# Five more filler products on TensorE ahead of the first running sum of a fused linear-attention and low-rank-mixer kernel

## The chip, the cores and the metric

The kernel runs on one NeuronCore of one Trainium2 chip. The metric is the device time of one execution in microseconds. Before the change, three timed runs gave 158.94, 158.34 and 158.42 us, so the median is 158.42 us.

## The reference

The reference is two layers in a row. The first is a gated linear attention over 4 batches, 8 heads, 768 time steps and a head size of 48:

```
state = alpha[:, :, t, :, None] * state + einsum('bhd,bhe->bhde', k[:, :, t], v[:, :, t])
y[:, :, t] = einsum('bhd,bhde->bhe', q[:, :, t], state)
```

Its output, with the heads side by side, is x of shape 4 x 768 x 384. The second layer is a mixer with a low rank over time and an MLP over channels:

```
h = x.transpose(0, 2, 1) @ U @ V          # rank 32 over the 768 time steps
u = x + h.transpose(0, 2, 1)
out = u + maximum(u @ w_ch1, 0) @ w_ch2   # 384 -> 1536 -> 384
```

## The kernel before, in words

Time is cut into chunks of 128 steps, six for each batch. In a chunk the recurrence over time becomes products. ScalarE (ACT) takes the logarithm of alpha (line 380), TensorE (PE) adds the logarithms up along time with triangular matrices (the running sum, f_cum, lines 387 to 399), ACT takes the exponentials of the sum and of its negative (lines 403 to 405), and GpSimd (POOL) or VectorE (DVE) scale k and q by these (line 411). PE then transposes k and q (line 428), ACT or DVE copy the transposed tiles out of PSUM (lines 277 and 279), PE forms the scores (line 452), DVE masks them (line 463), PE forms the state (lines 478 and 486) and the output y (lines 525 and 535). Batch 0 and most of batch 1 work on pairs of chunks in this way; the others have the same steps at lines 551 to 687. After the six chunks of a batch come the low-rank mix (lines 702 to 736) and the two products of the MLP (lines 765 and 791), with their relu (lines 775 and 777) and the last addition (line 797). The running sum is five lines of products: 384 columns (line 389), twice 192 (lines 390 and 391), 8 (line 392) and four times 4 (line 396).

The order of all this is not that of the loops. The loops only register operations, and Plan.run (line 125) issues them in the order of a table of three letters for each entry: two letters for the number of the operation and one for the engine that does it. Each engine works through its own instructions in that order, and waits on the others through semaphores. The queue of a DMA is that of the engine named by the letter, SyncE (SP) or ACT, so an ACT instruction behind a DMA that ACT issues waits until that DMA has been issued. The loads of alpha, k, q and v (line 350) fill 40 slots, and the first of them go out on both queues in turn with the first instructions.

An entry that begins with "++" is not an operation. Its third letter is a count of fillers, A for 0, B for 1, and so on:

```
for _ in range(CODE.index(table[n + 2])):
    self.warm(x)
```

A filler (line 270) is a product of 128 x 128 by 128 x 512 that reads a tile of zeros, set by DVE at line 201, and writes a PSUM bank that nothing holds at that point of the table; nobody reads its result. Ten such products are spread over the first part of the kernel, each entry with a count of one. Two of these entries, numbers 1 and 10 of the table, stand ahead of entry 11, the running sum of the first chunk (operation 141). Between them lie loads on SP and ACT, the preload of ACT's table and the logarithm of the first alpha tile.

Of the kernel before, what the change touches and what calls it, by code (L numbers as in the profile page):

```python
# [13 lines left out]

CODE = "ABCDEFGHIJKLMNOPQRSTUVWXYZabcdefghijklmnopqrstuvwxyz0123456789+-"
TABLE = """
ArA++BAASAvSA-AA3SQPAAySAsSCLA++BCNPAtSAzA++BA5ACOACPAAwS++BCiADSAECAAxSBAACRGAuS++BCSGCjACQACkPA4SClA++BCmAA7ADUPDVADWA
A0SC5ACTPCoGCUPCWABDSDXAEEPEGAA6SCpDA9ACVDCxPC7P++BCnACMAC9AAFGC+ABBSDrAA2SCyDCqPCsDCaPBHSCbDCXPCzPEFAA8SCrPCYDDtPCtAA1S
CcPCZDCeP++BCdDC8ADYGDaPCuPDZDCfPEIGDcAC-GDTGCwDEKPEHAAJPDbPC0DBCABFSABSDhPGCAAKADwA++BChACvDDiPDdDDjDEJGDvADuAA+SDePDgD
AGPELPAHADkPEMDC1PDfDBEAENABGSC2PBLSC3DDyGD0PD2ABISCgDBJSBKSBPSGEPDlDC6GGGADIPDJPDKDEOPDxGDLPDAGGHAEDGDBPC4DDzPDnPERPEPD  # L20
# [836 lines left out]
```

## Time and profile before

| what | us |
|---|---|
| median of the three timed runs | 158.42 |
| lowest and highest of them | 158.34, 158.94 |
| span of the profiled execution, first to last instruction | 156.8 |
| PE busy in that span | 148.8 (95%) |
| DVE, ACT, POOL busy | 107.6, 90.0, 61.4 |

The profile gives no time of its execution beside the span; the median of the timed runs is 1.6 us above it. Times in the trace count from the first instruction. In a row of the timeline the first number is the start, the second the time from the start of the first instruction of the row to the end of the last, then come engine, line, operation and the tiles written and read, the number of instructions as x2, and in brackets how long the engine had stood idle and what released it. Products of PE overlap: the next one starts before the result of the one before is complete, so the distance between two starts says more of the pace than the duration of one.

### The profile page before, as it was taken

To read this page: it belongs to the slowest core of one execution; us is meant where nothing else is said; L and a number is where in the kernel's file an instruction comes from. 1 tells how busy PE (TensorE), PEld (TensorE's weight loads), DVE (VectorE), ACT (ScalarE), POOL (GpSimd) and SP (SyncE) were. 2 spreads that over 40 slices of the span, in tenths; PEclk is the share of its full clock that TensorE was granted. 3 is DMA by queue.
4 is the path that set the end of the run, shared out by engine and by line. 5 is a ranking of instruction groups with operands and counts; after the bars stand their busy time and mean duration, and the time that the engine had idled before them with its cause. 6 is when DMAs were issued, how large, how long until landed. Compare 5 with 4: busy or idle time off the path is not lost.

```text
span 156.8 us, 4413 instructions
## 1 busy us (share of the span) xinstructions
PE 148.8 (95%) x1715; PEld 97.7 (62%) x1715; DVE 107.6 (69%) x236; ACT 90.0 (57%) x234; POOL 61.4 (39%) x95
## 2 busy tenths in 40 slices
PE   2878999999999999999999999999999999999992
PEld 0456678666767656666668666665667555556662
DVE  6038899987899628816588976885989580673162
ACT  3678889986978272999958585379232202450000
POOL 8285995756088600136679261052623000000000
PEclk9999999999999999999999999999999999999999
DMA  5999999999988989989989996897976346345625
GB/s 145 319 323 326 268 301 313 344 265 268 280 239 193 270 161 191 189 169 211 208 169 214 134 222 119 169 181 145 176 144 151 105 87 139 127 129 151 199 100 201
DMA packets 98291, 31.53 MB, mean 201 GB/s; under 512 B 91968, under 2 KB 98240, under 8 KB 98272
## 3 DMA queue, kind: packets, MB, share of 16 engines
q1 hardware_dynamic: 92464, 29.11, 80.6%
q10 hardware_dynamic: 5808, 2.16, 5.2%
q8 instruction: 13, 0.21, 0.6%
q14 instruction: 6, 0.05, 0.1%
HBM read 23.79 MB, written 4.72 MB: 182 GB/s over the span
## 4 chain that ended last, share of the span: by engine, by line
PE 84%; DMA 8%; DVE 4%; ACT 1%; issue 1%; ACTq 0%; DVEq 0%
PE ps L791 30%; PE ps L765 29%; DMA io<-in_alpha_dram 8%; PE ps L716 3%; PE ps L620 3%; PE ps L592 2%; PE ps L687 2%; PE ps L428 2%; PE ps L535 2%; PE ps L558 2%; PE ps L682 1%; PE ps L736 1%; PE ps L452 1%; PE ps L643 1%; PE ps L702 1%; DVE rkq L411 1%
## 5 line engine op out<-in xcount | busy, mean ns | idle before, releaser
L791 PE MATMUL ps<-w_sb,h1t 128*128 128x384 bf16 (+2 forms) x300 | 53.1, 319 | 0.0
L765 PE MATMUL ps<-uT,w_sb 128*128 128x384 bf16 x288 | 51.0, 326 | 0.1
L775 ACT ACTIVATE h1t<-ps 128x384 bf16<-128x384 f32 x58 | 27.2, 509 | 19.1 <-PE ps L765 19.0
L791 PEld LDWEIGHTS <-h1t 128*128 128x128 bf16 x300 | 27.3, 97 | 15.9 <-issue 0.6
L765 PEld LDWEIGHTS <-w_sb 128*128 128x128 bf16 x288 | 27.0, 98 | 16.3 <-issue 0.4
L777 DVE TENSOR_SCALAR h1t<-ps 128x384 bf16<-128x384 f32 x38 | 20.1, 552 | 19.4 <-PE ps L765 15.9
L579 POOL TENSOR_TENSOR rkq<-io,aa 128x384 bf16<-128x384 f32 x12 | 11.7, 975 | 23.0 <-ACT aa L569 13.2
L630 DVE TENSOR_TENSOR pm<-ps,maskc 128x512 bf16<-128x512 f32 x28 | 17.7, 681 | 2.8 <-PE ps L620 2.8
L717 DVE TENSOR_TENSOR ub<-xb,ps 128x384 bf16<-128x384 bf16 x24 | 12.2, 549 | 6.9 <-PE ps L716 6.9
L797 DVE TENSOR_TENSOR io<-ub,ps 128x384 f32<-128x384 bf16 (+2 forms) x25 | 12.9, 531 | 3.7 <-PE ps L791 3.6
L277 ACT CAST xb<-ps 128x192 bf16<-128x192 f32 (+1 forms) x21 | 8.2, 393 | 10.6 <-PE ps L687 7.9
L463 DVE TENSOR_TENSOR pm<-ps,maskp 128x512 bf16<-128x512 f32 x20 | 13.2, 682 | 0.5 <-PE ps L452 0.2
L277 ACT COPY kqt<-ps 128x512 bf16<-128x512 bf16 x18 | 10.5, 608 | 1.6 <-PE ps L428 0.8
L579 POOL TENSOR_TENSOR rkq<-io,ai 128x384 bf16<-128x384 f32 x9 | 8.2, 914 | 6.9 <-PE ps L643 3.9
L411 POOL TENSOR_TENSOR rkq<-io,ai 128x384 bf16<-128x384 f32 x9 | 8.5, 945 | 6.1 <-ACT lt L380 3.1
L568 ACT ACTIVATE ai<-ps 128x384 bf16<-128x384 f32 x14 | 7.0, 502 | 5.6 <-PE ps L560 3.1
L654 POOL TENSOR_TENSOR st<-sm,tot 128x384 bf16<-128x384 f32 x8 | 6.9, 868 | 8.2 <-DVE sm L670 8.0
L571 ACT ACTIVATE tot<-ps,off 128x4 f32<-128x4 f32 x22 | 5.6, 279 | 5.3 <-PE ps L560 3.4
L279 DVE COPY kqt<-ps 128x512 bf16<-128x512 bf16 x18 | 7.3, 417 | 1.4 <-PE ps L592 0.9
L428 PE MATMUL ps<-ident,rkq 128*128 128x128 bf16 x80 | 8.0, 228 | 0.1
L281 POOL CAST w_sb<-h1t 128x384 bf16<-128x384 f32 x14 | 6.8, 516 | 2.9 <-DMA h1t<-in_moe_w_ch_dram 2.9
L411 POOL TENSOR_TENSOR rkq<-io,aa 128x384 bf16<-128x384 f32 x7 | 6.4, 910 | 3.4 <-ACT aa L404 2.3
(111 smaller groups left out, 224.5 us busy)
## 6 DMA issues: line engine op xcount, KB each, us to landing
io<-in_v_dram SPq DMA_DIRECT2D x22, 192.0 KB, 4.1
io<-in_q_dram SPq DMA_DIRECT2D x22, 192.0 KB, 4.4
io<-in_k_dram SPq DMA_DIRECT2D x21, 192.0 KB, 4.0
io<-in_alpha_dram SPq DMA_DIRECT2D x20, 192.0 KB, 4.3
out_dram<-io SPq DMA_DIRECT2D x13, 192.0 KB, 2.0
h1t<-in_moe_w_ch_dram SPq DMA_DIRECT2D x4, 576.0 KB, 6.0
h1t<-in_moe_w_ch_dram SPq DMA_DIRECT2D x3, 768.0 KB, 6.6
out_dram<-io SPq DMA_DIRECT2D x20, 96.0 KB, 2.2
```

What stands on the lines that cost most here:

```text
L277: nc.scalar.copy(dst, src)
L411: eng.tensor_tensor(jh(dst()[:, :, 0:D]), raw(a), jh(x()), op=ALU.mult)
L428: nc.tensor.matmul(dst, lhsT=ring()[:, HP * j + 2 * a : HP * j + 2 * a + 2, :].rearrange("t h w -> t (h w)"), rhs=ident, start=True, stop= ...
L463: nc.vector.tensor_tensor(dst, s2, maskp.to_broadcast([C, 2, 2, C]), op=ALU.mult)
L579: eng.tensor_tensor(dst()[:, :, 0:D], a(), x(), op=ALU.mult)
L630: nc.vector.tensor_tensor(pm()[:, :, par, :], s2, maskc.to_broadcast([C, HP, C]), op=ALU.mult)
L717: P.add(f"u {b}.{c}", lambda e, c=c, hb=hb: nc.vector.tensor_tensor(ub()[:, c, :], xb()[:, c, :], hb()[:, 0:DM], op=ALU.add), r=[hb] + xk( ...
L765: nc.tensor.matmul(hb()[:, 0:TW], lhsT=w1_sb[:, ct, jt * 128 : (jt + 1) * 128], rhs=u_half(uT, ct, tt, b in QUEUE_U), start=(ct == 0), sto ...
L775: nc.scalar.activation(dst, hb()[:, 0:TW], AF.Relu)
L777: nc.vector.tensor_scalar_max(dst, hb()[:, 0:TW], 0.0)
L791: nc.tensor.matmul(hb()[:, 0 : hi - lo], lhsT=h1()[:, jt, c * C : (c + 1) * C], rhs=w2_sb[:, jt, lo:hi], start=(jt == 0), stop=(jt == NJ - 1),
L797: P.add(f"out_{hi - lo} {b}.{c}", lambda e, hb=hb, lo=lo, hi=hi: nc.vector.tensor_tensor(flat(ou)[:, lo:hi], ub()[:, c, lo:hi], hb()[:, 0 ...
```

## The change

One letter of the table changes, the count of entry 1 from B (1) to G (6). PE therefore issues six fillers there in place of one, and with the one of entry 10 seven in place of two, ahead of the first running sum. Entries, order, engines, slots and every other count stay.

```
 TABLE = """
-ArA++BAASAvSA-AA3SQPAAySAsSCLA++BCNPAtSAzA++BA5ACOACPAAwS
...
+ArA++GAASAvSA-AA3SQPAAySAsSCLA++BCNPAtSAzA++BA5ACOACPAAwS
...
```

More of the change, by code (lines that the diff above doesn't have):

```diff
@@ L16 @@
 TABLE = """
-ArA++BAASAvSA-AA3SQPAAySAsSCLA++BCNPAtSAzA++BA5ACOACPAAwS++BCiADSAECAAxSBAACRGAuS++BCSGCjACQACkPA4SClA++BCmAA7ADUPDVADWA
+ArA++GAASAvSA-AA3SQPAAySAsSCLA++BCNPAtSAzA++BA5ACOACPAAwS++BCiADSAECAAxSBAACRGAuS++BCSGCjACQACkPA4SClA++BCmAA7ADUPDVADWA
 A0SC5ACTPCoGCUPCWABDSDXAEEPEGAA6SCpDA9ACVDCxPC7P++BCnACMAC9AAFGC+ABBSDrAA2SCyDCqPCsDCaPBHSCbDCXPCzPEFAA8SCrPCYDDtPCtAA1S
```

## The prediction

> **What bounds the kernel now.** I read the chain of waits first, then the timeline of PE around the added products, then the other engines' timelines at the places where PE waits, and last the busy times by stretch.
>
> ```profile
> span 156.8 us, 4413 instructions
> PE   2878999999999999999999999999999999999992
> PEclk9999999999999999999999999999999999999999
> PE 84%; DMA 8%; DVE 4%; ACT 1%; issue 1%; ACTq 0%; DVEq 0%
> ```
>
> PE is the bound of the kernel as a whole, with 84% of the chain. But the change sits in the first slices, where PE's digits are lowest, so what it is worth is read from there. There the chain is this, in order of time:
>
> ```profile
> 0.73 2.96 DMA io<-in_alpha_dram
> 3.73 4.70 DMA io<-in_alpha_dram
> 8.45 0.37 ACTq L350
> 8.98 4.45 DMA io<-in_alpha_dram
> 13.45 0.03 ACT lt L380
> 13.88 0.47 ACT ai L403
> 14.36 0.48 ACT kqt L277
> 14.88 0.38 PE ps L270
> ```
>
> Three loads of alpha follow one another. The load that starts at 8.98 is held back by an issue on ACT's queue at 8.45, which went out when the load before it had landed (3.73 + 4.70 = 8.43). No piece of PE's work is on the chain before 14.88. PE's own view of the same time:
>
> ```profile
> 1.19 1.04 PE L270 MATMUL ps<-h1t 128*128 128x512 bf16 x2 [1.19 <-DVE h1t L201]
> 4.30 0.48 PE L389 MATMUL ps<-lt,upto 128*128 128x384 bf16 x1 [2.07 <-ACT lt L380]
> 5.07 1.44 PE L270 MATMUL ps<-h1t 128*128 128x512 bf16 x3
> 6.58 0.48 PE L389 MATMUL ps<-lt,upto 128*128 128x384 bf16 x1
> 7.35 0.59 PE L270 MATMUL ps<-h1t 128*128 128x512 bf16 x1
> 7.73 0.53 PE L389 MATMUL ps<-lt,upto 128*128 128x384 bf16 x1
> 8.05 0.37 PE L390 MATMUL ps<-lt,below 128*128 128x192 bf16 x1
> 8.55 1.25 PE L428 MATMUL ps<-ident,rkq 128*128 128x128 bf16 x8
> 9.59 0.48 PE L389 MATMUL ps<-lt,upto 128*128 128x384 bf16 x1
> 9.91 0.25 PE L390 MATMUL ps<-lt,below 128*128 128x192 bf16 x1
> 9.99 0.25 PE L391 MATMUL ps<-lt,upto 128*128 128x192 bf16 x1
> 10.88 0.34 PE L486 MATMUL ps<-rv,rkq 64*128 64x96 bf16 x8 [0.54 <-POOL rkq L411]
> 11.44 0.32 PE L389 MATMUL ps<-lt,upto 128*128 128x384 bf16 x1 [0.21 <-ACT lt L380]
> 11.60 0.24 PE L390 MATMUL ps<-lt,below 128*128 128x192 bf16 x1
> 11.91 0.38 PE L270 MATMUL ps<-h1t 128*128 128x512 bf16 x1
> 12.13 0.38 PE L428 MATMUL ps<-ident,rkq 128*128 128x128 bf16 x4
> 12.84 0.34 PE L486 MATMUL ps<-rv,rkq 64*128 64x96 bf16 x8 [0.33 <-ACT rv L277]
> 14.03 0.32 PE L389 MATMUL ps<-lt,upto 128*128 128x384 bf16 x1
> ```
>
> Two things are to be seen. First, PE's pace doubles at 9.9. The 384 columns of line 389 take 0.32 from start to next start at 7.73 (to 8.05) and 0.16 at 11.44 (to 11.60); the 192 columns of line 390 take 0.08 at 9.91 (to 9.99). The clock digits of the page show 9 in every slice and hide this; the spacing is what I go by. Second, after 9.9 PE waits three times in three microseconds, for POOL, for the logarithm and for a cast of v on ACT. It isn't the engine that is late there. The ones that are:
>
> ```profile
> 5.25 0.49 ACT L403 ACTIVATE ai<-ps 128x384 bf16<-128x384 f32 x1 [1.00 <-PE ps L396]
> 6.00 1.35 ACT L380 ACTIVATE lt<-io 128x384 bf16<-128x384 f32 x3
> 8.86 0.51 ACT L277 CAST rv<-io 128x384 bf16<-128x384 f32 x1 [1.52 <-DMA io<-in_alpha_dram]
> 13.45 0.52 ACT L380 ACTIVATE lt<-io 128x384 bf16<-128x384 f32 x1 [0.21 <-DMA io<-in_alpha_dram]
> 9.91 0.91 POOL L411 TENSOR_TENSOR rkq<-io,ai 128x384 bf16<-128x384 f32 x1 [0.78 <-ACT ai L403]
> ```
>
> ACT ends its three logarithms at 7.35 and then stands until the issue at 8.45 lets it go on at 8.86. From there POOL waits for ACT, and PE for POOL and ACT. The stretches, 3.4 us wide (a width of my choice that parts the time at the change of pace), and the end of the kernel:
>
> ```profile
> 3.07:6.48 3.41, 2.18 (x11) 0.99 (x11) 0.93 (x8) 1.76 (x5) 1.21 (x6) 1.00 1.14 313
> 6.49:9.89 3.40, 3.28 (x27) 2.20 (x26) 0.00 (x0) 1.88 (x7) 1.77 (x2) 1.00 1.17 323
> 9.91:13.31 3.40, 2.32 (x52) 1.83 (x51) 2.03 (x5) 3.33 (x11) 2.92 (x3) 1.00 1.17 324
> 153.26:156.67 3.41, 0.72 (x12) 0.53 (x9) 0.86 (x2) 0.00 (x0) 0.00 (x0) 1.00 0.56 200
> 156.70:156.78 0.08, 0.00 (x0) 0.00 (x0) 0.00 (x0) 0.00 (x0) 0.00 (x0) 0.50 0.00 0
> ```
>
> The columns are the stretch and its length, then busy time of PE, of PE's weight load, DVE, ACT and POOL, the granted clock, the DMA share and GB/s. ACT is busy 3.33 of 3.40 us between 9.91 and 13.31, and the DMAs move 323 to 324 GB/s on both sides of the change of pace. So this start is set by loads and, from 8.86 on, by ACT.
>
> **The change part by part.**
>
> *The five products.* At the slow pace 384 columns take 0.32, so 512 take 0.32 x 512 / 384 = 0.43. Two products from 1.19 leave PE free at 1.19 + 2 x 0.43 = 2.05; seven at 1.19 + 7 x 0.43 = 4.20. The first running sum starts at 4.30 because the logarithm is ready then, so 0.10 is left: 5 x 0.43 = 2.15 us of new work in an idle gap. Cost to the sum: 0. The bounds: should the sum have to wait for the seventh result (the lone filler at 7.35 takes 0.59, so 1.19 + 6 x 0.43 + 0.59 = 4.36), it starts 0.06 late. Exponentials and logarithms on ACT would shift by as much, ending at 7.41, still 1.04 ahead of the issue at 8.45; without that cover it would cost 0.06. The products issue no DMA and add no wait, and their bank and their tile of zeros are those of the old ones.
>
> *The pace of what follows.* The change of pace at 9.9 comes after a stretch in which PE was busy 3.28 of 3.40 us, and not after one with 2.18 of 3.41. With five more products the second becomes 2.18 plus the filled part of the gap (3.07 to 4.20, 1.13), about 3.3, as full as the one that was followed by the fast pace. I take it that the pace doubles some 3.4 us earlier, near 6.5. What that takes from PE: the running sums at 6.58 and 7.73 last 0.77 (to 7.35) and 0.82 (to 8.55), against 0.47 at 11.44 (to 11.91): 0.65 saved. The filler lasts 0.38 (7.35 to 7.73) against 0.22 (11.91 to 12.13): 0.16. Eight transposes last 1.04 (8.55 to 9.59); at half of it 0.52 is saved. The 384 columns at 9.59: 0.16. Together 1.5 us of PE time. The bounds are 0 (pace unchanged) and 2.8, half of the 5.6 us between 4.30 and 9.91.
>
> *Where that goes.* None of it reaches the end, because of the line at 10.88: there PE stands 0.54 for POOL's scaled k. POOL got its exponential late (0.78 idle at 9.91), since ACT was stopped until 8.86 by the load of alpha. ACT's input from PE at that time, the running sum of the second pair, is there at 7.35 already at the slow pace. So PE's idle time before 10.88 grows from 0.54 to about 2.0, while the start at 10.88 stays, and with it 11.44, 12.84 and 14.03. Of the 1.5 us the path gets 0. Without the cover it would get all of it.
>
> *The sum.* 156.8 + 0 + 0 = 156.8 us of span. The timed median lies 158.42 - 156.8 = 1.6 above the span, for which the profile gives nothing; added back, it makes 158.4.
>
> **The rivals.**
>
> *The early pace reaches the end.* If some step after 13.45 ends last because of PE's slow work before 9.9, up to 1.5 us come back: 158.4 - 1.5 = 156.9, at the outer bound 155.6. For it speaks that PE is 84% of the chain, so any PE time truly freed is worth its full length. Against it stand the three waits after 9.9, each on an engine that is behind the loads. A timed run in which the fast pace comes later than 9.9 would bear it out better: then the slow products would fall on 11.44 to 14, where the idle times are only 0.21 and 0.33. The Trainium skill, "TensorE: Matmul & The Clock Gate", Part 1, gives this a reason: there the array's clock is halved until one window of about 3.4 us was busy, and the windows run freely, not from the kernel's start. By that rule the moment differs from run to run; the trace's doubling after a full stretch agrees, and one execution can't show the spread.
>
> *The fast pace is lost again: slower.* Faster products leave PE idler between 6.5 and 10.9, and the slow pace could return. At the end of the trace the granted clock is 0.50 after a stretch in which PE was busy 0.72 of 3.41 us; it stayed full through one with 2.32. After the change the stretch from 6.49 has about 3.28 - 1.5 = 1.8, between the two and nearer to 2.32, so I expect it kept. The point of decision is somewhere between 0.72 and 1.8. If it is lost, the products from 9.91 to 13.31 take up to twice their 2.32 us; idle times of 0.54 + 0.21 + 0.33 = 1.08 cover part, and 2.32 - 1.08 = 1.2 remain: 159.6. The skill's same page, section "HAM oscillation", warns of gaps over about 3.4 us before the next burst; the longest gap after 6.5 would here be the 2.0 us before 10.88, so by that rule the clock stays.
>
> *The products do not bring the pace forward.* They multiply zeros, and no row shows that such products count towards the change of pace; the stretch with 3.28 was mostly real work. Then the pace still doubles at about 9.9, and the time is 158.4 again.
>
> **How the numbers follow.** The forecast (earlier pace, all of it hidden) gets 0.70, the fast end 0.10, the loss of the pace 0.08, no earlier pace 0.12. The first and the last give the same time, 158.4. A measurement of this kernel tells about 0.5%, 0.79 us, from no change, so faster means below 157.6 and slower above 159.2. The chances are 0.10 faster, 0.82 the same, 0.08 slower. The three runs before spread from 158.34 to 158.94, and a median of a few can move by about that. For the range I take that spread on both sides, with the unknown 0.06 above, and go a little way towards the rivals, whose ends at 156.9 and 159.6 hold 0.18: 157.7 to 159.1.
>
> **What the profile after would show.** Seven products from 1.19 with starts 0.43 apart and the first running sum still near 4.30 would confirm the first step. The 384 columns of the sums near 6.58 or 7.73 at 0.16 in place of 0.32 would confirm the second; 0.32 up to 9.9 would bear out the last rival. For the third, PE's idle time before the products of line 486 should grow to near 2 us with their start still close to 10.9, and the load at 13.43 and the logarithm at 13.45 should stay in place. A return to 0.32 between 9.9 and 14, for instance at 11.44, would show the slower rival. A span below 156.0, with the logarithm at 13.45 or the work behind it earlier, would make the prediction wrong, and so would a span above 157.6.

## The result and the profile after

The changed kernel takes 159.27 us in the median of 20 runs (157.86 to 160.44), the kernel before beside it 158.34 us (157.64 to 160.25). The ratio is 1.0054 with a 95% interval of 1.0028 to 1.0079: slower by half a per cent, where no change was forecast. Two later comparisons of the same kernel gave smaller ratios, 1.0005 (0.9974 to 1.0036) and 1.0024 (0.9991 to 1.0057). Why they differ is part of the explanation. The ratios leave out executions far above the fastest of their kernel; the medians and counts in this document are over all executions.

The profiled execution of after took 158.85 us, less than the median of its kernel; by its clock, 0.999, it is one of 4 of the 20 without the loss that is described below. From its page:

```profile
span 157.0 us, 4423 instructions
PE   6958999899999999999999999999999999999992
...
PEclk9999999999999999999999999999999999999999
```

And the chain of waits, up to 16 us:

```profile
8.64 4.45 DMA io<-in_alpha_dram
...
13.11 0.03 ACT lt L380
13.14 0.40 issue
13.54 0.47 ACT ai L403
14.01 0.48 ACT kqt L277
...
14.54 0.38 PE ps L270
```

PE's digit in the first slice rises from 2 to 6, and the chain at the start is still that of the loads: a load of alpha, its logarithm, the exponential, the copy, and then PE. All of it is 0.34 us earlier than in the trace of before, because the load ahead of it landed at 8.08 and not at 8.43. That is no effect of the change: in traces of other executions, with two fillers and with none, it landed at 8.33 and 7.99. PE's timeline of the same execution:

```profile
1.19 3.17 PE L270 MATMUL ps<-h1t 128*128 128x512 bf16 x7 [1.19 <-DVE h1t L201]
4.31 0.48 PE L389 MATMUL ps<-lt,upto 128*128 128x384 bf16 x1
...
6.59 0.32 PE L389 MATMUL ps<-lt,upto 128*128 128x384 bf16 x1
6.75 0.24 PE L390 MATMUL ps<-lt,below 128*128 128x192 bf16 x1
...
8.01 0.40 PE L428 MATMUL ps<-ident,rkq 128*128 128x128 bf16 x4 [0.15 <-POOL rkq L411]
8.87 0.40 PE L428 MATMUL ps<-ident,rkq 128*128 128x128 bf16 x4 [0.47 <-POOL rkq L411]
...
10.54 0.34 PE L486 MATMUL ps<-rv,rkq 64*128 64x96 bf16 x8 [0.84 <-POOL rkq L411]
```

Seven products run from 1.19, the first running sum starts at 4.31 as before, and the 384 columns at 6.59 take 0.16 (to 6.75): the fast pace is there 3.4 us earlier. The time won is idle time ahead of 8.01, 8.87 and 10.54.

In this trace the change does what was forecast, and nothing in it is slow. What is slow shows in the list of all executions, which gives the mean granted clock of each. It takes only a few values, and the time goes with them. For after (its 20 runs and the 24 of the two repetitions below), and for the 93 runs of before beside the experiments, whose clocks are listed too:

| mean granted clock | after: runs, mean us | before: runs, mean us |
|---|---|---|
| 0.997 to 1.000 | 13, 158.22 | 84, 158.39 |
| 0.987 or 0.989 | 27, 159.19 | 6, 159.42 |
| 0.976 to 0.979 | 4, 160.04 | 3, 160.25 |

A mean lower by 0.011 over a span of 157 us is 0.011 x 157 / 0.5, some 3.4 us at half clock, and a trace below shows such a stretch. So, by this estimate, 31 of 44 executions of the changed kernel have one or two stretches of 3.4 us at half clock, each worth some 0.9 us, and 9 of 93 executions of before. Executions without one take the same time in both kernels within the noise. The mean over all is 158.98 against 158.52, 0.46 us or 0.3% more; how large the difference comes out in one comparison depends on how many of its executions were hit: 16 of 20 in the first, 8 and 7 of 12 in the others.

### The profile page after: what moved, and what is told of

It reads as the page before. It is cut to its first block, busy times and chain, and to the rows that moved or that the text cites. A ratio compares the mean times of both kernels' runs of the same rounds, so it can differ in the third digit from the quotient of the medians.

```text
span 157.0 us, 4423 instructions
## 1 busy us (share of the span) xinstructions
PE 149.7 (95%) x1720; PEld 97.9 (62%) x1720; DVE 107.5 (68%) x236; ACT 90.2 (57%) x234; POOL 61.6 (39%) x95
## 4 chain that ended last, share of the span: by engine, by line
PE 86%; DMA 7%; DVE 2%; ACT 1%; issue 1%; ACTq 0%; DVEq 0%
PE ps L791 30%; PE ps L765 30%; DMA io<-in_alpha_dram 7%; PE ps L716 3%; PE ps L620 3%; PE ps L592 2%; PE ps L428 2%; PE ps L687 2%; PE ps L535 2%; PE ps L558 2%; PE ps L682 1%; PE ps L736 1%; PE ps L452 1%; PE ps L643 1%; PE ps L702 1%
## 5 line engine op out<-in xcount | busy, mean ns | idle before, releaser
L579 POOL TENSOR_TENSOR rkq<-io,aa 128x384 bf16<-128x384 f32 x12 | 11.6, 974 | 24.0 <-ACT aa L569 14.2
L270 PE MATMUL ps<-h1t 128*128 128x512 bf16 x15 | 6.5, 543 | 1.4 <-DVE h1t L201 1.2
```

The lines of the kernel that those rows point to most:

```text
L579: eng.tensor_tensor(dst()[:, :, 0:D], a(), x(), op=ALU.mult)
```

## The experiments

All comparisons of a row are with the kernel before on the same chip. Theory A is the rival of the prediction by which the fast pace is lost again for want of work on PE. Theory B is a fall of the clock from outside the kernel, and theory C that each added filler carries its own share of the loss. "Lost" stands for a mean granted clock of 0.989 or less.

**The changed kernel again (no edit).**

> The changed kernel once more, for a trace of an execution like most of the 20. Of these, 4 have a mean granted clock of 0.997 or more and take 157.86 to 158.85 us, 13 have 0.987 to 0.989 (158.65 to 160.44) and 3 have 0.976 or 0.977 (159.93 to 160.11); 0.011 of a span of 157 us is 3.4 us at half clock. Theory A (the fast pace comes earlier, and PE is then so idle between 6.5 and 10.5 us that it is lost again for one stretch of 3.4 us, in some executions for two): the trace shows the 384-column sums at 0.16, then a stretch at 0.32 somewhere between 6 and 20 us, the clock of most executions is near 0.989, and the median is about 159.3. Theory B (the clock falls for a reason outside the kernel, at any place): the low stretch lies somewhere else, or the executions of the kernel before show the same share of 0.989.

Measured: 158.70 us in the median, 8 of 12 lost, these 158.87 us in the mean and the other four 158.17. Its profiled execution is a lost one. The trace records when a granted clock begins: here full at 4.23, half at 11.06, full again at 14.47, so that each stretch of 3.4 us can be cut where the hardware changed. Busy times by stretch (columns as in the prediction), and below them the row of the granted clock on its page:

```profile
0.83:4.23 3.40, 3.04 (x8) 1.06 (x9) 2.56 (x23) 1.81 (x2) 3.18 (x12) 1.00 0.77 193
4.23:7.64 3.41, 2.48 (x29) 1.56 (x27) 0.00 (x0) 2.11 (x5) 0.78 (x2) 1.00 1.17 321
7.65:11.04 3.39, 1.61 (x25) 1.23 (x26) 1.15 (x2) 2.60 (x8) 2.59 (x4) 1.00 1.17 323
11.06:14.46 3.40, 3.40 (x43) 2.40 (x43) 1.85 (x6) 2.65 (x9) 1.85 (x3) 0.50 1.17 323
14.47:17.87 3.40, 3.23 (x60) 2.07 (x57) 3.10 (x8) 2.81 (x9) 2.68 (x4) 1.00 1.17 320
```

```profile
PEclk9996999999999999999999999999999999999999
```

Here the fast pace came at 4.2, after a stretch that held almost nothing but the seven fillers. It was kept after a stretch with PE busy 2.48 us and lost after one with 1.61: from 11.06 to 14.46 the granted clock is 0.50. PE's timeline and the chain of this execution show what that does:

```profile
4.18 0.34 PE L389 MATMUL ps<-lt,upto 128*128 128x384 bf16 x1
4.35 0.25 PE L390 MATMUL ps<-lt,below 128*128 128x192 bf16 x1
...
10.45 0.34 PE L486 MATMUL ps<-rv,rkq 64*128 64x96 bf16 x8 [0.88 <-POOL rkq L411]
11.01 0.47 PE L389 MATMUL ps<-lt,upto 128*128 128x384 bf16 x1 [0.22 <-ACT lt L380]
11.26 0.37 PE L390 MATMUL ps<-lt,below 128*128 128x192 bf16 x1
...
14.28 0.42 PE L389 MATMUL ps<-lt,upto 128*128 128x384 bf16 x1
```

```profile
10.54 0.42 ACT lt L380
11.01 0.47 PE ps L389
...
11.90 0.45 PE ps L270
12.35 0.43 PE ps L428 x4
12.78 0.43 PE ps L486 x8
13.21 0.57 PE ps L452 x12
13.78 0.28 PE ps L478
14.06 0.43 PE ps L428 x4
...
15.16 0.38 PE ps L270
```

From 11.01 the chain is PE's. The third load of alpha and its logarithm, which carried the chain in after, have gone from it. The filler at the end of both chains starts at 15.16 where after has 14.54: 0.62 us later, although the loads here are 0.08 us earlier (landing at 8.00 against 8.08). So in this trace one lost stretch costs about 0.6 to 0.7 us at that point; between the two groups of this run's executions it is 158.87 - 158.17 = 0.7.

**The kernel before, with its clocks (no edit).**

> The kernel before, run as a kernel of its own so that each execution lists its clock. Theory A: nearly all executions have 0.997 or more, and the few at 159.2 us and above (3 of 20 so far) have 0.989 or less; median about 158.3. Theory B: most executions have 0.989, as with the changed kernel.

Measured: 158.10 us, 1 of 12 lost, and that one took 159.37 us, the longest of the twelve. The kernel without the change loses the pace rarely, on the same chip and in the same comparison as the 8 of 12. Theory B falls.

**Fillers in the idle gaps behind the early pace.**

Two fillers go between the transposes of k and of q of the first pair (behind entry 42, operation 147), and three ahead of the first state product (entry 54, operation 177):

```
 CTP
+++C
...
+++D
 CxP
```

> The changed kernel with five more fillers in the two idle gaps of PE behind the early change of pace: two between the transposes of k and of q of the first pair (0.47 us idle before 8.87 in the trace of after) and three ahead of the first state product (0.84 us idle before 10.54). Five fillers at the fast pace are 5 x 0.22 = 1.1 us. Theory A: the clock stays at 0.997 or more in nearly all executions and the median returns to about 158.3 (158.0 to 158.6). Theory B: the clocks are spread as with the changed kernel and the median stays at 159.3; if instead the mere number of fillers costs time, 159.5 or more.

Measured: 158.43 us, ratio 1.0000 (0.9966 to 1.0034), 0 of 12 lost. Its busy times by stretch, and two rows of PE's timeline:

```profile
1.92:5.33 3.41, 3.41 (x15) 1.43 (x14) 1.73 (x17) 1.76 (x3) 2.29 (x8) 1.00 1.06 290
5.33:8.74 3.41, 2.62 (x26) 1.45 (x24) 0.00 (x0) 2.18 (x6) 1.66 (x2) 1.00 1.17 323
8.75:12.15 3.40, 2.90 (x36) 1.83 (x37) 1.25 (x3) 3.40 (x12) 2.64 (x4) 1.00 1.17 323
```

```profile
8.28 0.59 PE L270 MATMUL ps<-h1t 128*128 128x512 bf16 x2
...
10.58 0.34 PE L486 MATMUL ps<-rv,rkq 64*128 64x96 bf16 x8 [0.18 <-POOL rkq L411]
```

The pace comes early here too, at 5.3, and the stretches behind it hold 2.62 and 2.90 us of PE's time. The idle time ahead of the state product has shrunk from 0.84 to 0.18, with its start at 10.58. The trace has 20 weight loads of the fillers but only 19 products: the record of the first of the three ahead of the state product is missing, so PE's last stretch holds more than 2.90. With the gaps filled, the seven early fillers cost nothing that the interval shows, and they bring nothing either. Three of the twelve took 159.5 to 159.8 us at a clock of 0.999 or 1.000; no trace shows what made these long (7 of the 84 of before without a loss are above 159 us too).

**None ahead of the first running sum.**

```
 (the table before, entries 1 and 10)
-++B
+++A
```

> The kernel before without its two fillers ahead of the first running sum (seven in the changed kernel). Theory A: the pace doubles at about 9.9 us as before, since the stretch from 6.5 to 9.9 is as full, the clock stays at 0.997 or more in nearly all executions, and the time is 158.3 (158.0 to 158.7). Theory B: clocks as in the other kernels, no difference in either direction.

Measured: 158.41 us, ratio 0.9988 (0.9956 to 1.002), 1 of 10 lost. Leaving out the two fillers of the kernel before costs nothing that shows.

**Four, and five, ahead of the first running sum.**

```
 (the table before, entry 1)
-++B
+++D      # four in all; E for five
```

> Four fillers ahead of the first running sum (two before, seven in the changed kernel). They end near 2.9 us and leave PE idle for about 1.3 us until 4.2. So far the fast pace followed stretches of 3.4 us with PE busy 3.04 or more, and not those with 2.45 or less. Theory A, refined (the early change of pace needs the idle gap closed; only then is PE fast and idle enough behind it to lose the pace): with 1.3 us of the gap left open no stretch that begins ahead of 3.5 is full enough, so the pace doubles at 7 us or later as in the kernel before, 11 or 12 of 12 executions keep a clock of 0.997 or more, and the median is 158.1 to 158.5. Theory C (each filler ahead of the sum adds a share of the loss): 2/5 of the way, so about a third of the executions at 0.989 and a median near 158.5 to 158.8.

> Five fillers ahead of the first running sum, between the four that lost the pace in none of 12 executions and the seven that lost it in 31 of 44. They end near 3.5 us and leave about 0.8 us idle until 4.2 to 4.3. Theory A: a stretch over the gap has PE busy some 2.6 of 3.4 us, between the 2.48 after which the pace did not double and the 3.04 after which it did, so the result places the point: 0 to 2 of 12 lost and a median of 158.1 to 158.5 if the gap still holds the pace back, 6 or more and 158.7 to 159.2 if not. Theory C (each filler adds its share): 3/5 of 31/44, about 5 of 12, median 158.5 to 158.8.

Measured: four give 158.20 us, ratio 0.9994 (0.9976 to 1.0011), 0 of 12 lost; five give 158.33 us, ratio 1.0005 (0.9972 to 1.0038), 1 of 12. So the loss doesn't grow filler by filler, and theory C falls. It sets in between five and seven, where the idle gap ahead of the first sum closes; six were not run. The trace with four has no record of the clock at all, and such an execution reads as 1.000; its timeline shows no return to the slow pace up to 20 us, and 11 of its 12 executions took less than 158.6 us, while the one of 160.57 can't be told. In the timeline with four the gap is 1.15 us and the sums at 6.50 and 7.65 keep the slow pace; with five, the stretch over the gap had PE busy 2.67 us and the fast pace came only after the next. (The 2.48 of the expectation belongs to a stretch that kept the fast pace; the one that did not bring it, in the second trace of before, held 2.45.) The rows with four, then those with five:

```profile
4.22 0.48 PE L389 MATMUL ps<-lt,upto 128*128 128x384 bf16 x1 [1.15 <-ACT lt L380]
...
7.65 0.53 PE L389 MATMUL ps<-lt,upto 128*128 128x384 bf16 x1
7.97 0.37 PE L390 MATMUL ps<-lt,below 128*128 128x192 bf16 x1
...
9.12 0.33 PE L389 MATMUL ps<-lt,upto 128*128 128x384 bf16 x1
```

```profile
1.82:5.22 3.40, 2.67 (x13) 1.13 (x12) 1.80 (x17) 1.81 (x3) 2.39 (x8) 1.00 1.07 282
5.23:8.63 3.40, 3.33 (x22) 1.77 (x21) 0.00 (x0) 2.31 (x6) 1.76 (x2) 1.00 1.17 323
```

**One filler in the gap.** In place of the five of the gap experiment, a single "++B" ahead of entry 54.

> The changed kernel with a single filler (0.22 us) ahead of the first state product. The stretch after which the pace was lost had PE busy 1.61 of 3.39 us; the emptiest after which it was kept had 2.22 of 3.41. One filler makes 1.83 of the first. Theory A: if the point of decision lies above 1.83, the share of executions at 0.989 stays near that of the changed kernel (24 of 32 so far at 0.989 or below) and the median near 158.7 to 159.2; if it lies below, the share falls to a few of 12 and the median to 158.4. Either result narrows the point. Theory B (the five gap fillers helped by chance of the executions): no change in the share.

Measured: 158.36 us, ratio 0.9984 (0.9951 to 1.0018), 4 of 12 lost, two of them with two stretches. One filler of 0.22 us takes the share from 31 of 44 to about half of that, so it lies near the point of decision and doesn't settle its place. The trace of this run kept the pace.

**The kernel before with the gap fillers.** The same five fillers in the two gaps, with two ahead of the first sum.

> The kernel before with the same five fillers in the two gaps, two between the transposes of the first pair and three ahead of the first state product, but only two ahead of the first running sum. Theory A: the late change of pace (7 to 10.6 us) stays; the few executions of the kernel before that lose a stretch (4 of 47 with 0.989 or below so far) are gone, and the median is 158.1 to 158.4, the same as before; if the fillers at the slow pace (0.43 us each) delay the state product beyond its wait of 0.54 us, up to 0.5 us slower, 158.8. A time below 157.9 would make it better than both kernels.

Measured: 158.41 us, ratio 1.0002 (0.9979 to 1.0025), 0 of 12 lost. Nothing is won over the kernel before; its own rare losses are too few to show in 12.

**The changed kernel a third time (no edit).**

> The changed kernel once more beside these three, on their chip. Theory A: 7 to 10 of 12 executions at 0.989 or below, these 0.6 to 1.0 us above the others of the same kernel, median 158.6 to 159.3; the others equal to the kernel before within 0.2 us. If nearly all were at 0.997 or more and the median still above 158.6, theory A would fall.

Measured: 158.66 us, 7 of 12 lost; the six at 0.989 took 159.21 us in the mean, the five others 158.18. Its profiled execution kept the pace, through these two stretches:

```profile
5.82:9.22 3.40, 2.12 (x24) 1.28 (x23) 0.00 (x0) 1.95 (x5) 1.77 (x2) 1.00 1.17 323
9.23:12.64 3.41, 2.20 (x33) 1.72 (x34) 1.46 (x3) 3.41 (x13) 2.77 (x3) 1.00 1.17 324
```

So the point below which the pace was lost lies between 1.61 and 2.12 us of 3.4 in these traces. Where the stretches begin is what differs: in this same trace the 3.41 us from 8.00 hold 1.59, but no stretch of this execution began there.

**Less work behind the early pace.** The opposite of the gap fillers: two later fillers of the changed kernel taken out.

```
 (the changed kernel's table, entries 34 and 56)
-++B
+++A
```

> The changed kernel without two later fillers: the one between the second and the third running sum (7.04 us in the trace of after) and the one behind the running sum at 11.10 (11.57 us). PE is 0.2 us idler in each of the two stretches behind the early change of pace. Theory A (the pace is lost for want of work there): the share of executions with a mean clock of 0.989 or below rises from 31 of 44 to 10 or more of 12, more of them at 0.977 (two stretches), and the median goes to 159.1 to 159.8. A theory that only the early change of pace itself counts: the share stays at 7 to 9 of 12, the median at 158.7 to 159.2. If fewer fillers help: below 158.5.

Measured: 160.14 us in the median, 11 of 12 lost: two with one stretch (159.34 us in the mean), four with two, and five with a clock of 0.957, which by the same estimate is four stretches (161.95 us). The twelfth kept the pace and took 157.82 us. Against the changed kernel's medians of 159.27, 158.70 and 158.66, two fillers fewer cost 0.9 to 1.5 us; those runs were on other chips or in other comparisons, but the kernel before had 158.33 to 158.35 beside each. The stretches of the profiled execution, and the row of the clock on its page:

```profile
4.46:7.86 3.40, 2.15 (x27) 1.40 (x25) 0.00 (x0) 2.11 (x5) 0.50 (x1) 1.00 1.17 322
7.88:11.27 3.39, 1.57 (x24) 1.20 (x25) 0.92 (x2) 2.41 (x8) 2.65 (x4) 1.00 1.17 322
11.29:14.69 3.40, 3.21 (x42) 2.39 (x42) 2.17 (x6) 2.90 (x11) 1.86 (x3) 0.50 1.17 323
14.70:18.10 3.40, 3.40 (x53) 2.45 (x51) 2.82 (x5) 2.00 (x5) 2.97 (x4) 0.50 1.16 309
```

```profile
PEclk9995799999999999999999999999999999999999
```

The pace was lost after 1.57 us of work. It didn't return after the next stretch, though PE was busy 3.21 of 3.40 us in it, and only after one with 3.40. With more fillers in the gaps, 0 of 12; with one, 4 of 12; with none, 31 of 44; with two taken away, 11 of 12: the loss follows the work on PE behind the early pace. Theory A stands.

The fillers in the gaps also shorten the longest gap, so a rule on the length of one gap is a rival. The traces speak against it, though no run separates the two: gaps of 0.84 and 0.82 us ahead of the state product stand in the profiled executions of after and of its third comparison, which kept the pace, and 0.83 and 0.80 in those with four and five fillers, which lost it in 0 and 1 of 12. The two lost stretches hold gaps of 0.88 and 0.82 (the second also the end of one of 1.01). By work the kept and the lost stretches lie further apart, 2.12 and more against 1.61 and less.

## Why the prediction was wrong

*The five products: right.* They were to end at 4.20 and the first sum to start at 4.30; it starts at 4.31.

*The pace of what follows: right in this execution.* Near 6.5 was forecast; at 6.59 the columns run at 0.16. That the moment came so close is chance: in the other traces with seven fillers it lies between 4.2 and 6.7. That products of zeros might not count was a rival with 0.12; the stretch from 0.83 to 4.23, filled with them, was followed by the fast pace.

*Where the gain goes: right in kind.* The path gets 0: executions that keep the pace take 158.22 us, those of before 158.39, a difference that the noise covers. The wait before 10.88 was to grow to about 2.0 us; it is 0.84, with 0.47 and 0.15 more ahead of the transposes, 1.46 in all. The working overlooked that the transposes wait for POOL too once PE is fast.

*The loss of the pace: this step failed.* The prediction had the mechanism as its slower rival, with 0.08, and the sentence that failed is "between the two and nearer to 2.32, so I expect it kept". Two errors stand in it. It took the position of the stretches from the one trace of before and worked out the work of one of them, 1.8 us from 6.49; in after that stretch held 2.52, 0.7 more than worked out, and kept the pace:

```profile
6.49:9.89 3.40, 2.52 (x34) 1.82 (x32) 0.00 (x0) 2.24 (x8) 2.10 (x3) 1.00 1.17 323
```

But the position differs from execution to execution: in the six traces with seven fillers the fast pace began between 4.2 and 6.7, in the two of the kernel before at 9.9 and 10.4. In the lost execution a stretch began at 7.65 and held 1.61, and the text itself had 2.0 us of idle time ahead of 10.88. And the rows on which the text rested allow a point of decision anywhere between 0.72 and 2.32; it was put below 1.8, which is the conclusion itself. It lies between 1.61 and 2.12. So the loss, which had a chance of 0.08, is there in 31 of 44 executions.

*Its price* was put at 1.2 us; the groups of executions give 159.19 - 158.22 = 0.97. The range ended at 159.1, and the median of 159.27 lies above it. The medians of the two repetitions, 158.70 and 158.66, lie inside: on which side the number fell depended on how many executions were hit, 16 of 20 or 8 and 7 of 12. That is chance; the step was wrong in all three.

For this step the prediction also drew on the Trainium skill, "TensorE: Matmul & The Clock Gate", section "HAM oscillation": the rule there is that no idle gap should be longer than about 3.4 us, and the prediction took from it that a shorter one keeps the clock. The traces don't agree with that: the longest gap in the stretch ahead of the loss was 0.88 us, and the clock fell after 1.61 us of work in 3.39. The measurement decides. Part 1 of that page of the Trainium skill says that the windows run freely and last about 3.4 us, and that the moment of the change differs from run to run; with that the traces agree, with 3.40 us from 11.06 to 14.46 at half clock and a first change anywhere from 4.2 to 6.7. The prediction drew on it and didn't draw the conclusion for the slower rival.

*What stays open:* what exactly the hardware counts. PE's busy time in the profile isn't quite it, since a stretch with 3.04 us of it brought the fast pace in one trace and a stretch with 3.21 us did not in another. Nor did any trace catch the changed kernel with two lost stretches, so their price is known from the groups of executions alone. And since a trace without a record of the clock reads as 1.000, the counts of lost executions are lower bounds.

## What to carry to other kernels

Work that only wakes an engine up may need enough work behind it to keep it awake: here the filled gap at the start opened gaps behind it, and the half clock came back where PE was no longer covered by the loads. Before filling an idle gap, look for what ends last at that place; where loads do, a faster engine there buys only idle time. And when a change acts on a state that differs between executions, one trace can't show it; sort all executions by their granted clock first.

## What was not expected of the hardware

- TensorE in use half of the time can lose its clock: the stretch with 1.61 of 3.39 us busy was followed by 3.4 us at half clock, with no gap above 0.88 us.
- The lost pace can last: with two fillers fewer, one trace stays at half clock for two stretches, from 11.29 to 18.10 us, and the mean clock of 0.957 in five of twelve executions is that of four, 161.95 us against 157.82 for the one with none.
- Products of zeros count: seven of them and little else were followed by the fast pace at 4.2 us.
- The clock digits of the page show 9 before the first change of pace, though the spacing of products there is twice as long (in before 0.32 us for 384 columns ahead of it, 0.16 behind it); the trace's records of the clock begin with that change, in before at 9.9 us.
